# Memory denominators as 32 columns, the gate's last product through PSUM, the head mask from GpSimd ramps, and a new order

## The chip, the cores and the metric

The kernel runs on one core of a Trainium2 chip. Its time is the device time of one execution, in microseconds, and a kernel's time is the median of its runs. The engines are TensorE (PE, with its weight loads as PEld), VectorE (DVE), ScalarE (ACT), GpSimd (POOL) and SyncE (SP), which here only issues DMAs.

## What is computed

A block of two parts over 2048 rows of 512 values, in float32: attention with a compressed memory, then a gated FFN, each behind a layer norm and with a residual.

```python
x = A_x
h = x + _A_ref(_layernorm(x), A_wq, A_wk, A_wv, A_wo, A_beta)
h2 = h + _B_ref(_layernorm(h), B_w_gate, B_w_up, B_w_down)
```

The attention has 32 heads of 16 columns and 4 segments of 512 rows. Within a segment it is causal softmax attention. From the segments before it each head keeps a 16 x 16 memory M and a vector z:

```python
num = jnp.einsum("bhld,bhde->bhle", pq, M)          # pq = phi(q)
den = jnp.einsum("bhld,bhd->bhl", pq, z)[..., None] + 1e-6
o = g * (num / den) + (1.0 - g) * a_dot             # g = sigmoid(beta), one for each head
M = M + jnp.einsum("bhld,bhle->bhde", pk, vs)       # pk = phi(k)
z = z + jnp.einsum("bhld->bhd", pk)
```

The FFN is `(gelu(x @ w_gate) * (x @ w_up)) @ w_down`, with 1376 inner columns and the tanh form of gelu.

## The kernel before

**Units.** 8 heads (a chunk c of 128 columns) in one segment s are a unit: 16 units, each of two halves of 4 heads. For a unit, `qkv` projects Q and K (L888, for the first unit L898), splits them into a high part (ACT, L983) and a low part (DVE, L985), and copies both by DMA into the tiles stq and stk (L996, L1002), where a head's rows lie in the interleaved form that the passes read. `vproj` makes V for two chunks (L927, L940 for the first) in the tile vaug.

**Two passes.** For each half `pass_a` multiplies Q by K (L1123) and lets DVE take each row's largest value from PSUM (L1133, into nm). GpSimd splits these values into high and low (L1147, L1148), DVE turns them into rows by four 32 x 32 transposes (L1154, `turn`), and a DMA writes them into stq, so that `pass_b`'s product (L1177) comes with the maximum taken off. ACT exponentiates (L1183), GpSimd cuts the diagonal blocks (L1191), and PE multiplies by V in 32-column tiles (L1205).

**Memory.** `mup` (L1037, PE in 32-column tiles) forms pk times v and the sum of pk for a unit. `mask` (L1048, L1051) spreads that over the heads into the tile mb, multiplying by a constant head mask, mmask. Columns 0 to 127 of mb hold the memory; columns 128 to 159 hold the vector z of 8 heads, each repeated 4 times. GpSimd adds the unit before (L1058). `mem` uses it in segments 1 to 3, 12 times in all: `den` (L1073) multiplies mb's last 32 columns, as weights, by pq in four products of 128 columns, `inv` adds 1e-6, inverts and multiplies by the gate (L1079 to L1081), every fourth row of the result goes to DRAM and comes back spread over 128 partitions, and the numerators (L1091) are multiplied by it (L1096).

**Constants.** mmask is made at the start: two GpSimd ramps (L606, L608), and on DVE a copy to integers (L615), a bitwise and (L616), three subtractions over 32 partitions each (L618) and one comparison (L620).

**FFN.** Weights and activations are combined in blocks so that 7 products (L1466) stand for 8. `geglu` runs for two halves s of the rows: ACT squares (L1484), DVE L1486, ACT tanh (L1488), DVE L1490 (tanh + 1, times the gate), DVE L1492 (half of that, times u), then ACT and GpSimd split the result and `down` multiplies by w_down (L1530), added up by DVE (L1538). For s = 0 u is a PSUM bank; for s = 1 it is a tile in SBUF.

**The order.** Every step is recorded as an operation of one engine with a planned length. A table of 4741 numbers, ORDER, gives the order in which all of them are issued; buffers come from pools in that order (all 8 PSUM banks are one pool, 35 row tiles another), and the planner refuses an order in which none is free. A planned length decides nothing at run time: it served to lay out the order. For DVE it is `n / 960 + 0.072` us. Each engine, and SP's queue, works strictly in its order.

The functions that the change touches:

Of the kernel before, what the change touches and what calls it, by code (L numbers as in the profile page):

```python
# [1632 lines left out]
```

## Time and profile before

| | us |
|---|---|
| median of 3 runs | 765.69 (765.08 to 765.71) |
| the profiled execution | 764.84 |
| its span, first to last instruction | 762.9 |
| PE, PEld busy | 739.2, 583.7 |
| DVE, ACT, POOL busy | 610.5, 503.3, 479.6 |

The profile is of one execution. The page gives shares and groups; the trace behind it answers for windows, for the timeline, for waits (who waited for whom) and for the chain, which is followed back from the last instruction through whatever released each one. Matmuls overlap, so the mean of one is longer than what it takes of PE; the busy time of a group, divided by its steps, is the better price. An entry such as `[4.46 <-DMA stq<-slot]` is idle time ahead of an instruction and what ended it. Line numbers are those of the kernel before; in the changed kernel the same lines stand two lower up to L1035 (L985 is L983, L1037 is L1035) and one or two higher behind `inv` (L1123 is L1124, L1154 is L1155, L1492 is L1494).

### The profile page before, as it was taken

The page shows a single profiled execution, that of the slowest core. Times are in us where ns is not written, and L with a number is a line of the kernel's source. Part 1 is how long each engine was busy: PE and PEld are TensorE (multiplying, and loading weights), DVE is VectorE, ACT ScalarE, POOL GpSimd, SP SyncE. Part 2 cuts the span into 40 slices and gives each one's busy share as a digit, 9 for nine tenths or more (in the row PEclk, how much of TensorE's full clock was granted, in tenths as well). Part 3 has the DMA queues.
Part 4 walks back from the last instruction along what each step waited for, and adds up shares of the span by engine and source line. Part 5 has one row for each costly group of instructions (what it writes and reads, how often), then busy time and mean ns, then how long its engine had stood idle before and what let it go on. Part 6 is the DMA issues. An engine that isn't in the chain of part 4 may idle for free.

```text
span 762.9 us, 17952 instructions
## 1 busy us (share of the span) xinstructions
PE 739.2 (97%) x6126; PEld 583.7 (77%) x6126; DVE 610.5 (80%) x1922; ACT 503.3 (66%) x1004; POOL 479.6 (63%) x748
## 2 busy tenths in 40 slices
PE   7799999999999999999999999999999999999998
PEld 6688778776878777676667788788887878888886
DVE  6899889999998899999997554875678765665576
ACT  5688887787876777867766456866586455464450
POOL 6244554544545565778676689866998378768731
PEclk9899999999999999999999999999999999999999
DMA  6465657546656677776667684442544252000002
GB/s 247 125 183 137 163 154 192 151 123 196 184 149 192 166 204 198 187 212 209 169 191 232 191 277 147 120 101 48 150 124 128 56 152 79 2 1 0 1 1 110
DMA packets 88394, 107.85 MB, mean 141 GB/s; under 512 B 29824, under 2 KB 40624, under 8 KB 88304
## 3 DMA queue, kind: packets, MB, share of 16 engines
q1 hardware_dynamic: 88000, 106.32, 49.0%
q8 instruction: 48, 0.79, 0.5%
q10 hardware_dynamic: 304, 0.39, 0.2%
q14 instruction: 42, 0.34, 0.2%
HBM read 57.02 MB, written 23.53 MB: 106 GB/s over the span
## 4 chain that ended last, share of the span: by engine, by line
PE 74%; DVE 17%; issue 3%; ACT 3%; DMA 2%; SPq 1%; POOL 0%; DVEq 0%; ACTq 0%; POOLq 0%
PE bank L1466 26%; PE bank L1530 14%; PE bank L888 8%; PE bank L1205 7%; PE bank L927 4%; PE bank L1123 4%; PE bank L1177 4%; DVE aside L1133 3%; PE bank L1278 3%; DVE bank L1133 3%; DVE mx L1154 1%; PE bank L1285 1%; PE bank L1091 1%; DVE slot L985 1%; DVE nm L1133 1%
## 5 line engine op out<-in xcount | busy, mean ns | idle before, releaser
L1183 ACT ACTIVATE row<-bank 128x512 f32<-128x512 f32 x306 | 164.7, 604 | 38.6 <-PE bank L1177 26.9
L1191 POOL TENSOR_SCALAR_AFFINE_SELECT row<-row 128x256 f32<-128x256 f32 (+1 forms) x306 | 105.2, 367 | 99.9 <-ACT row L1183 87.9
L1133 DVE CUSTOM_DVE_ANT_0 aside<-bank,amask 128x128 f32<-128x128 f32 (+2 forms) x384 | 142.0, 419 | 7.3 <-PE bank L1123 4.7
L888 PE MATMUL bank<-slot,slot 64*128 64x512 f32 x720 | 117.3, 408 | 0.0
L1466 PE MATMUL bank<-slot,slot 128*128 128x512 f32 (+1 forms) x381 | 103.3, 391 | 1.1 <-DVE row L1538 1.1
L1123 PE MATMUL bank<-stk,stq 64*128 64x256 f32 (+3 forms) x512 | 88.3, 337 | 6.8 <-DMA stq<-slot 4.5
L1133 DVE CUSTOM_DVE_ANT_0 bank<-bank,amask 128x512 f32<-128x512 f32 x128 | 86.4, 710 | 5.4 <-PE bank L1123 5.0
L1177 PE MATMUL bank<-stq,stk 64*128 64x512 f32 (+3 forms) x512 | 85.6, 337 | 1.4 <-DVE nm L1133 0.3
L1466 PEld LDWEIGHTS bank<-slot,slot 128*128 128x128 f32 (+1 forms) x381 | 69.9, 184 | 18.3 <-DVE row L1538 2.0
L1205 PE MATMUL bank<-row,vaug 128*32 128x128 f32 (+3 forms) x976 | 78.1, 437 | 3.6 <-DVE nm L1133 0.9
L888 PEld LDWEIGHTS bank<-slot,slot 64*128 64x128 f32 x720 | 76.0, 188 | 6.6 <-issue 0.8
L1538 DVE TENSOR_TENSOR row<-row,bank 128x512 f32<-128x512 f32 (+1 forms) x91 | 60.1, 676 | 22.6 <-PE bank L1530 22.5
L1123 PEld LDWEIGHTS bank<-stk,stq 64*128 64x128 f32 x512 | 60.0, 188 | 22.9 <-DVE nm L1133 7.7
L1436 POOL TENSOR_TENSOR slot<-row,slot 128x512 fp32r<-128x512 f32 (+3 forms) x56 | 63.4, 1141 | 21.9 <-ACT slot L1434 21.9
L1177 PEld LDWEIGHTS bank<-stq,stk 64*128 64x128 f32 x512 | 58.0, 184 | 16.8 <-DVE nm L1133 5.7
L1530 PE MATMUL bank<-slot,slot 128*128 128x512 f32 (+1 forms) x252 | 67.6, 391 | 0.9 <-DVE row L1490 0.6
L668 POOL TENSOR_TENSOR slot<-row,slot 128x512 fp32r<-128x512 f32 (+1 forms) x34 | 44.0, 1293 | 28.1 <-ACT slot L663 27.8
L1205 PEld LDWEIGHTS bank<-row,vaug 128*32 128x32 f32 x976 | 30.6, 109 | 39.2 <-issue 31.9
L1530 PEld LDWEIGHTS bank<-slot,slot 128*128 128x128 f32 (+1 forms) x252 | 47.1, 188 | 12.0 <-DVE row L1490 1.0
L927 PE MATMUL bank<-slot,slot 64*128 64x256 f32 x672 | 54.9, 284 | 0.0
L927 PEld LDWEIGHTS bank<-slot,slot 64*128 64x128 f32 x672 | 49.5, 186 | 2.0 <-issue 0.8
L1133 DVE DVE_READ_ACCUMULATOR2_ANT nm<- 128x1 f32 x512 | 50.0, 98 | 0.0
(254 smaller groups left out, 1660.5 us busy)
## 6 DMA issues: line engine op xcount, KB each, us to landing
stq<-slot SPq DMA_DIRECT2D x96, 128.0 KB
stk<-slot SPq DMA_DIRECT2D x94, 128.0 KB
row<-x SPq DMA_DIRECT2D x32, 256.0 KB
pv_dram<-row SPq DMA_DIRECT2D x31, 256.0 KB
row<-r_dram SPq DMA_DIRECT2D x27, 256.0 KB
row<-h_dram SPq DMA_DIRECT2D x22, 256.0 KB
row<-wg SPq DMA_DIRECT2D x17, 256.0 KB
row<-wd SPq DMA_DIRECT2D x17, 256.0 KB
```

The costliest lines, as they stand in the source:

```text
L888: return nc.tensor.matmul(pm[i].t, w[i].t[rows_of(r), wi, dc * P:(dc + 1) * P], XT[s][dc].t[rows_of(r), xi, :], start=(dc, wi, xi, ph) == ...
L927: return nc.tensor.matmul(pms[n].t[:, 256 * t:256 * t + 256], XT[s][dc].t[rows_of(r), xi, t0:t0 + P], whl[wi].t[rows_of(r), dc // 2, 256 * ...
L1123: nc.tensor.matmul(sa.t[:, c0:c0 + w], sq.t[own, p, i * P:(i + 1) * P], sk.t[own, p, 0:w], start=True, stop=True, tile_position=(64 * a, 0 ...
L1133: nc.vector.tensor_tensor_reduce(out=(sa.t[:, c0:c0 + w] if i > 2 else aside[:, turns[0]:turns[0] + w]), in0=sa.t[:, c0:c0 + w], in1=amask ...
L1177: nc.tensor.matmul(sc.t[:, c0:c0 + D - q0], sk.t[own, p, q0:q0 + P], sq.t[own, p, q0:D], start=True, stop=True, tile_position=(64 * a, 0), ...
L1183: act(w, prio, lambda sc=sc, e=e: nc.scalar.activation(e.t[:, :w], sc.t[:, :w], AF.Exp), [sc, vtab], [e])
L1191: nc.gpsimd.affine_select(v, v, pattern=pat + [[1, P]], compare_op=OP.is_ge, fill=0.0, base=0, channel_multiplier=-1)
L1205: nc.tensor.matmul(pv.t[32 * n:32 * n + 32, kb * P:D], va.t[:, 136 * kb + 17 * j:136 * kb + 17 * j + 32], e.t[:, lo:lo + D - kb * P], star ...
L1436: pool(0.14 + 2.13e-3 * (hi - lo), prio, lambda: nc.gpsimd.tensor_tensor(v.t[:, 1, :hi - lo], r.t[:, lo:hi], v.t[:, 0, :hi - lo].bitcast(F ...
L1466: nc.tensor.matmul(dst.t[:w], v.t[:, wi, c0 + j * w:c0 + (j + 1) * w], b[bk][j].t[:, xi, :], start=first and j == 0 and n == 0, stop=j == ...
L1530: nc.tensor.matmul(pm.t[:, cs], HH[p, f, s].t[:w, hi, t * P:(t + 1) * P], v.t[:w, wi, cs], start=f == fl[0] and n == 0, stop=f == fl[-1] a ...
L1538: dve(W_, prio, lambda a=a, pm=pm, cs=cs, to=to: nc.vector.tensor_tensor(to.t[:, cs], a.t[:, cs], pm.t[:, cs], op=OP.add), [pm, a], [to])
```

## The change

Denominators. mb has 8 columns for z in place of 32, and the product is turned round: pq is the weights, in 16 tiles of 32 columns, mb's 8 columns are what streams, and the result stands with the rows of x on the partitions and 4 x 8 columns beside each other. `inv` works on these 32 columns, multiplies by a gate that is now spread over all partitions (8 columns for each chunk), and turns the result by one transpose for the write to DRAM.

```diff
-    PZ = Pool_(many("z", 1, [P, P]))
+    PZ = Pool_(many("z", 2, [P, 32]))
-    PMB = Pool_(many("mb", 7, [P, 160]))
+    PMB = Pool_(many("mb", 7, [P, 136]))
-    gt = sb("gt", [P, 2, NCH])
+    gt = sb("gt", [P, 9, NCH])
...
             for t in range(4):
-                nc.tensor.matmul(pd.t[32 * t:32 * t + 32, 0:P], mb.t[:, P:160],
-                                 pq.t[:, t * P:(t + 1) * P], start=True, stop=True,
-                                 tile_position=(0, 32 * t), skip_group_check=True)
-        pe(0.22, prio, den, [pq, mb], [pd], acq=[z], head=0.03, tail=0.02, mode="c")
+                for i in range(4):
+                    q0 = t * P + 32 * i
+                    nc.tensor.matmul(pd.t[32 * i:32 * i + 32, 8 * t:8 * t + 8], pq.t[:, q0:q0 + 32],
+                                     mb.t[:, P:136], start=True, stop=True,
+                                     tile_position=(0, 32 * i), skip_group_check=True)
+        pe(0.25, prio, den, [pq, mb], [pd], acq=[z], head=0.03, tail=0.02, mode="c")
...
-            nc.vector.tensor_scalar(pd.t[:, 0:P], pd.t[:, 0:P], 1e-6, None, op0=OP.add)
-            nc.vector.reciprocal(pd.t[:, 0:P], pd.t[:, 0:P])
-            nc.vector.tensor_scalar(z.t, pd.t[:, 0:P], gt[:, 1, c:c + 1], None, op0=OP.mult)
-        dve(1500, prio, inv, [pd, vgt], [pd, z])
+            d = pd.t[:, 0:32]
+            nc.vector.tensor_scalar(d, d, 1e-6, None, op0=OP.add)
+            nc.vector.reciprocal(d, d)
+            by_t = d.rearrange("p (t j) -> p t j", t=4)
+            nc.vector.tensor_tensor(by_t, by_t, gt[:, None, 1:9, c].to_broadcast([P, 4, 8]), op=OP.mult)
+            nc.vector.transpose(z.t, d.rearrange("p (t j) -> p j t", t=4))
+        dve(560, prio, inv, [pd, vgt], [pd, z])
```

`mask` writes 4 columns for z where it wrote 16, twice for each unit; the loads of the gate values and the write to DRAM change their shapes to match.

Head mask. GpSimd makes the second ramp in four pieces of 32 partitions, each with its own start, so the three subtractions go; the integers are kept in a PSUM bank (vs) in place of a row tile.

```diff
+    vs = Val(PD)
...
-        nc.gpsimd.iota(jid, pattern=[[1, 8], [0, 17]], base=0, channel_multiplier=0,
-                       allow_small_or_imprecise_dtypes=True)
+        for r in range(4):
+            jid = vj.t[32 * r:32 * r + 32, 0:136].rearrange("p (j e) -> p j e", e=17)
+            nc.gpsimd.iota(jid, pattern=[[1, 8], [0, 17]], base=-(r % 2 + 4 * (r // 2)), channel_multiplier=0,
+                           allow_small_or_imprecise_dtypes=True)
...
-        hidi = vj.t[:, 136:272].bitcast(I32)
-        nc.vector.tensor_copy(hidi, hid)
+        hidi = vs.t[:, 0:136].bitcast(I32)
+        nc.vector.tensor_copy(hidi, vh.t[:, 0:136])
         nc.vector.tensor_scalar(hidi, hidi, 1, None, op0=OP.bitwise_and)
-        for r in range(1, 4):
-            nc.vector.tensor_scalar(jid[32 * r:32 * r + 32], jid[32 * r:32 * r + 32],
-                                    -float(r % 2 + 4 * (r // 2)), None, op0=OP.add)
...
-    dve(1500, -9.5, c_mmask, [vh, vj], [vmmask, vh, vj])
+    dve(640, -9.5, c_mmask, [vh, vj], [vmmask, vs])
```

Gate. For s = 1 the product of tanh + 1 and the gate is written back into the gate's PSUM bank, and the last product reads it there; that bank is held until then.

```diff
+            r = g_ if s else e
             dve(D, prio, lambda: nc.vector.scalar_tensor_tensor(
-                e.t[:w], e.t[:w], 1.0, g_.t[:w], op0=OP.add, op1=OP.mult), [g_], [e])
+                r.t[:w], e.t[:w], 1.0, g_.t[:w], op0=OP.add, op1=OP.mult), [g_, e], [r])
             dve(D, prio, lambda: nc.vector.scalar_tensor_tensor(
-                e.t[:w], e.t[:w], 0.5, u_.t[:w], op0=OP.mult, op1=OP.mult), [u_], [e])
+                e.t[:w], r.t[:w], 0.5, u_.t[:w], op0=OP.mult, op1=OP.mult), [u_, r], [e])
```

Planned lengths and order. Beside the new steps above, the turn is planned at 760 for 330, a row transpose of `layer_norm` at 600 for 512, the copies into stq and stk at 155 KB for 128, and the whole of ORDER is laid out anew. Its numbers say nothing to a reader; this is its kind:

```diff
-        dve(330, prio, turn, [m2], [mx])
+        dve(760, prio, turn, [m2], [mx])
...
-    6, 10, 8, 12, 5, 9, 7, 11, 84, 0, 1, 75, 14, 15, 16, 18, 72, 73, 4, 771, 2, 970, 13, 81, 17, 19, 28, 74,
```

What it moves, at three places. The first is DVE at the start, behind the last low halves of the first segment's input. slot_79 and slot_80 (slot_81 and slot_82 after) are Q and K of the first unit, bn and mv the sums of the second segment's layer norm. Before:

```order
L615 CAST row_109<-row_108 128x136
L616 TENSOR_SCALAR row_109<-row_109 128x136
L618 TENSOR_SCALAR row_109<-row_109 32x136 x3
L620 SCALAR_TENSOR_TENSOR mmask<-row_109 128x136
L724 BN_STATS bn_157<-row_118 128x6
L725 BN_AGGR mv_159<-bn_157 128x2
L724 BN_STATS bn_157<-row_120 128x6
L725 BN_AGGR mv_159<-bn_157 128x2
L713 TENSOR_SCALAR mv_160<-bn_158 128x1
L716 TENSOR_SCALAR bn_158<-bn_158 128x1
L985 SCALAR_TENSOR_TENSOR slot_79<-bank_71,slot_79 128x512
L985 SCALAR_TENSOR_TENSOR slot_80<-bank_72,slot_80 128x512
```

And now, on the same engine, from the last low half of the input (L855; L857 before, where it stood ahead of the small L713, now L711) to those of Q and K:

```order
L711 TENSOR_SCALAR mv_161<-bn_159 128x1
L855 TENSOR_TENSOR slot_76<-bank_70,slot_76 128x512
L714 TENSOR_SCALAR bn_159<-bn_159 128x1
L722 BN_STATS bn_158<-row_110 128x6
L723 BN_AGGR mv_160<-bn_158 128x2
L722 BN_STATS bn_158<-row_118 128x6
L723 BN_AGGR mv_160<-bn_158 128x2
L722 BN_STATS bn_158<-row_114 128x6
L723 BN_AGGR mv_160<-bn_158 128x2
L983 SCALAR_TENSOR_TENSOR slot_81<-bank_71,slot_81 128x512
L983 SCALAR_TENSOR_TENSOR slot_82<-bank_72,slot_82 128x512
```

The head mask now follows after four rows more on the same engine, and behind it the first pass:

```order
L767 TENSOR_SCALAR bank_67<-mv_160 128x4
L616 CAST bank_68<-row_106 128x136
L617 TENSOR_SCALAR bank_68<-bank_68 128x136
L618 SCALAR_TENSOR_TENSOR mmask<-bank_68,row_107 128x136
L773 RECIPROCAL ln_166<-ln_165 128x4
```

The whole mask has gone from ahead of the low halves of Q and K to behind them, and takes three instructions for six; three statistics stand ahead of those low halves where two stood. On ACT's queue the first two copies of K into stk (L1002) stood behind the high halves of Q and K with two activations between, one of them L719, which waits for DVE; now three stand between, L661, L907 and L661.

The second place is DVE near the end of attention, at the last of the 12 inversions (bank_68 before, bank_66 after, are the denominators; mx is what the turn writes). Before:

```order
L1079 TENSOR_SCALAR bank_68<-bank_68 128x128
L1080 RECIPROCAL bank_68<-bank_68 128x128
L1081 TENSOR_SCALAR z_138<-bank_68,gt 128x128
L545 COPY tock<-bank_72 128x1
L1154 STREAM_TRANSPOSE mx_156<-mm_155 32x32 x4
L545 COPY tock<-bank_65 128x1
```

And now:

```order
L545 COPY tock<-bank_65 128x1
L1155 STREAM_TRANSPOSE mx_157<-mm_156 32x32 x4
L545 COPY tock<-bank_69 128x1
L1079 TENSOR_SCALAR bank_66<-bank_66 128x32
L1080 RECIPROCAL bank_66<-bank_66 128x32
L1082 TENSOR_TENSOR bank_66<-bank_66,gt 128x32
L1083 STREAM_TRANSPOSE z_139<-bank_66 128x32
```

The turn stood behind the inversion and now stands ahead of it; the inversion has 32 columns and one instruction more.

The third place is PE at the first denominators (mb is the memory, vaug is V). Before:

```order
L888 MATMUL bank_65<-slot_90,slot_84 128x512
L1123 MATMUL bank_70<-stk_95,stq_100 128x512
L1123 MATMUL bank_72<-stk_95,stq_100 128x512
L1073 MATMUL bank_67<-row_123,mb_145 32x128 x4
L1205 MATMUL bank_66<-row_101,vaug_140 32x512
```

And now:

```order
L1206 MATMUL bank_66<-row_122,vaug_141 32x256
L1206 MATMUL bank_66<-row_114,vaug_141 32x256
L1072 MATMUL bank_69<-mb_146,row_118 32x8 x16
L1035 MATMUL bank_68<-vaug_141,row_125 32x34 x16
L1206 MATMUL bank_72<-row_105,vaug_141 32x512
```

4 products of 128 columns became 16 of 8, with the operands in each other's place; here they stand among other products in 32-column tiles, where before they opened such a stretch. Over the whole program PE goes 43 times from 64-row tiles to 32-column tiles, and went 40 times before. In the FFN the two DVE rows of the gate (L1492 and L1494 in the changed kernel) stand directly behind each other in 15 of the 22 gated tiles of s = 1.

More of the change, by code (lines that the diff above doesn't have):

```diff
@@ L600, in infini_geglu @@
     vj = Val(PJ)
+    vs = Val(PD)
     def c_iota():
         hid = vh.t[:, 0:136].rearrange("p (j e) -> p j e", e=17)
-        jid = vj.t[:, 0:136].rearrange("p (j e) -> p j e", e=17)
         nc.gpsimd.iota(hid, pattern=[[0, 8], [0, 17]], base=0, channel_multiplier=1,
                        allow_small_or_imprecise_dtypes=True)
-        nc.gpsimd.iota(jid, pattern=[[1, 8], [0, 17]], base=0, channel_multiplier=0,
-                       allow_small_or_imprecise_dtypes=True)
-    pool(1.0, -9.5, c_iota, [], [vh, vj])
+        for r in range(4):
+            jid = vj.t[32 * r:32 * r + 32, 0:136].rearrange("p (j e) -> p j e", e=17)
+            nc.gpsimd.iota(jid, pattern=[[1, 8], [0, 17]], base=-(r % 2 + 4 * (r // 2)), channel_multiplier=0,
+                           allow_small_or_imprecise_dtypes=True)
+    pool(1.7, -9.5, c_iota, [], [vh, vj])
     def c_mmask():
-        hid, jid = vh.t[:, 0:136], vj.t[:, 0:136]
-        hidi = vj.t[:, 136:272].bitcast(I32)
-        nc.vector.tensor_copy(hidi, hid)
+        hidi = vs.t[:, 0:136].bitcast(I32)
+        nc.vector.tensor_copy(hidi, vh.t[:, 0:136])
         nc.vector.tensor_scalar(hidi, hidi, 1, None, op0=OP.bitwise_and)
-        for r in range(1, 4):
-            nc.vector.tensor_scalar(jid[32 * r:32 * r + 32], jid[32 * r:32 * r + 32],
-                                    -float(r % 2 + 4 * (r // 2)), None, op0=OP.add)
-        nc.vector.scalar_tensor_tensor(mmask.rearrange("p j e -> p (j e)"), hidi, 2.0, jid,
+        nc.vector.scalar_tensor_tensor(mmask.rearrange("p j e -> p (j e)"), hidi, 2.0, vj.t[:, 0:136],
                                        op0=OP.mult, op1=OP.is_equal)
-    dve(1500, -9.5, c_mmask, [vh, vj], [vmmask, vh, vj])
+    dve(640, -9.5, c_mmask, [vh, vj], [vmmask, vs])
     def c_ident():
@@ L830, in layer_norm @@
             q = Val(PN)
-            dve(D, prio, lambda t=t, q=q: nc.vector.transpose(q.t, rows[t].t), [rows[t]], [q])
+            dve(600, prio, lambda t=t, q=q: nc.vector.transpose(q.t, rows[t].t), [rows[t]], [q])
             for a in range(4):
@@ L997, in qkv @@
                                               hl.t[64 * h:64 * h + 64, part].bitcast(F32)),
-                            [hl] + zeros, [dst], kb=128, chain=True)
+                            [hl] + zeros, [dst], kb=155, chain=True)
                         continue
@@ L1005, in qkv @@
                     else:
-                        dma(moved + 0.2 + h, lambda move=move: move(nc.sync), [hl] + zeros, [dst], kb=128,
+                        dma(moved + 0.2 + h, lambda move=move: move(nc.sync), [hl] + zeros, [dst], kb=155,
                             chain=True)
@@ L1051, in mask @@
                 nc.vector.tensor_tensor(
-                    mb.t[:, P:160].rearrange("p (a b j r) -> p a b j r", a=2, b=2, j=2)[:, :, :, j],
-                    m[:, None, :, 16:17].to_broadcast([P, 2, 2, 4]),
-                    pick[:, :, :, 16:17].to_broadcast([P, 2, 2, 4]), op=OP.mult)
+                    mb.t[:, P:136].rearrange("p (a b j) -> p a b j", a=2, b=2)[:, :, :, j],
+                    m[:, None, :, 16].to_broadcast([P, 2, 2]), pick[:, :, :, 16], op=OP.mult)
         dve(330, later + 0.8, mask, [pu, vmmask], [mb])
@@ L1072, in den @@
             for t in range(4):
[L1073 to L1082 removed]
+                for i in range(4):
[4 more added lines that the diff above has]
+        pe(0.25, prio, den, [pq, mb], [pd], acq=[z], head=0.03, tail=0.02, mode="c")
+        def inv():
+            d = pd.t[:, 0:32]
[5 more added lines that the diff above has]
+        dve(560, prio, inv, [pd, vgt], [pd, z])
         dma(prio, lambda: nc.sync.dma_start(
[L1084 to L1085 removed]
+            r_dram[U, 1].rearrange("j (t i q) -> i (j t) q", t=4, i=4), z.t), [z], [vr], kb=16)
         om = OM[U] = Val(POM)
@@ L1376, in infini_geglu @@
     pool(0.1, 0.5, lambda: nc.gpsimd.memset(gt, 0.0), [], [vgt, vgz])
-    for i, ap in enumerate([[[0, 16], [NCH, 8], [1, NCH]], [[0, 4], [NCH, 8], [1, NCH]]]):
+    for i, ap in enumerate([[[0, 16], [NCH, 8], [1, NCH]], [[0, P], [1, 8 * NCH]]]):
         dma(1, lambda i=i, ap=ap: nc.sync.dma_start(
-            gt[0:P:4 if i else 1, i], bass.AP(tensor=beta.tensor, offset=beta.offset, ap=ap)), [*XT[1], vgz], [vgt],
+            (gt[:, 1:9] if i else gt[:, 0]), bass.AP(tensor=beta.tensor, offset=beta.offset, ap=ap)), [*XT[1], vgz], [vgt],
             kb=2, chain=True)
-    act(8, 1, lambda: nc.scalar.activation(gt, gt, AF.Exp, scale=-1.0), [vgt, vtab], [vgt])
+    act(36, 1, lambda: nc.scalar.activation(gt, gt, AF.Exp, scale=-1.0), [vgt, vtab], [vgt])
     def c_gate():
```

2 lines of the change are left out of this document (removed), and 507 rows, old and new, of the table ORDER.

## The prediction

> **What bounds the kernel now.** I read the page first: how busy each engine is, and which engines the chain that ended last runs through.
>
> ```profile
> PE 739.2 (97%) x6126; PEld 583.7 (77%) x6126; DVE 610.5 (80%) x1922; ACT 503.3 (66%) x1004; POOL 479.6 (63%) x748
> PE 74%; DVE 17%; issue 3%; ACT 3%; DMA 2%; SPq 1%; POOL 0%; DVEq 0%; ACTq 0%; POOLq 0%
> ```
>
> PE (TensorE) is busy for 739.2 of 762.9 us, so no more than 23.7 us of visible PE idle time can be won; DVE holds 17% of the chain. An average over stages hides where, so I cut the span into windows at the places where the program changes its nature: start, first head passes, attention, FFN (columns: the window, its length, then PE, PEld, DVE, ACT, POOL busy, granted clock, DMA share, GB/s).
>
> ```profile
> 0.00:24.00 24.00, 19.44 (x108) 16.46 (x108) 17.68 (x36) 11.28 (x24) 13.11 (x32) 1.00 0.57 203
> 24.00:28.00 4.00, 0.00 (x0) 0.00 (x0) 2.13 (x9) 3.66 (x13) 2.26 (x4) 0.79 0.91 211
> 28.00:34.00 6.00, 5.70 (x36) 5.12 (x38) 4.39 (x23) 4.75 (x9) 0.00 (x0) 0.57 0.78 233
> 34.00:60.00 26.00, 25.16 (x333) 20.97 (x331) 23.80 (x110) 21.18 (x46) 11.76 (x26) 1.00 0.53 147
> 60.00:400.00 340.00, 331.74 (x4018) 251.56 (x4014) 321.77 (x1348) 259.79 (x531) 198.28 (x438) 1.00 0.64 177
> 400.00:759.00 359.00, 356.86 (x1641) 289.42 (x1642) 239.94 (x400) 202.69 (x387) 254.21 (x250) 1.00 0.34 100
> ```
>
> Four readings. The FFN (400 to 759) is PE alone: 2.1 us idle, DVE at 67%. Attention (60 to 400) is nearly two-sided: PE 97.6%, DVE 321.77 of 340, 94.6%, so work taken off DVE counts there. From 34 to 60 DVE is at 92%. And between 24 and 28 PE does nothing, while the granted clock falls to 0.79 and then 0.57. The timeline shows what came before that gap and what ended it; its next to last row is of the chain.
>
> ```profile
> 14.47 0.16 DVE L713 TENSOR_SCALAR mv<-bn 128x1 f32<-128x1 f32 x1
> 14.61 0.93 DVE L615 CAST row<-row 128x136 int32<-128x136 f32 x1
> 15.57 1.22 DVE L616 TENSOR_SCALAR row<-row 128x136 int32<-128x136 int32 x1
> 16.80 3.92 DVE L618 TENSOR_SCALAR row<-row 32x136 f32<-32x136 f32 x3
> 17.92 5.91 PE L940 MATMUL bank<-slot,slot 128*128 128x256 f32 x48
> 17.89 1.09 ACT L983 ACTIVATE slot<-bank 128x512 fp32r<-128x512 f32 x2 [1.10 <-PE bank L898]
> 20.75 0.30 DVE L620 SCALAR_TENSOR_TENSOR mmask<-row 128x136 f32<-128x136 int32 x1
> 22.68 1.28 DVE L985 SCALAR_TENSOR_TENSOR slot<-bank,slot 128x512 fp32r<-128x512 f32 x2
> 24.63 3.54 DMA stq<-slot
> ...
> 28.30 1.33 PE L1123 MATMUL bank<-stk,stq 64*128 64x384 f32 x8 [4.46 <-DMA stq<-slot]
> ```
>
> The head mask (L615 to L620) holds DVE from 14.61 to 21.05, 6.4 us, three subtractions on 32 partitions taking 3.92 of it. ACT has the high halves of Q and K at 18.98, but DVE forms the low halves (L985) only at 22.68; SP's copies into stq queue behind them, the last is issued at 24.63 and lands 3.54 us later. PE ends the V projection at 23.83 and waits 4.46 us.
>
> **The change, part by part.**
>
> *Head mask.* DVE loses the three subtractions and its first two steps go to a PSUM bank; the new order also puts all of it behind the low halves. Ahead of these now stand three statistics of the next layer norm, as cheap as here:
>
> ```profile
> 21.69 0.18 DVE L725 BATCH_NORM_AGGREGATE mv<-bn 128x2 f32<-128x6 f32 x1
> 21.79 0.66 DVE L724 BATCH_NORM_STATS2 bn<-row 128x6 f32<-128x512 f32 x1
> 22.97 0.61 ACTq L1002 DMA_DIRECT2D stk<-slot  x1
> 9.22 0.50 POOL L873 COPY tick<-row 128x1 f32<-128x1 f32 x1 [5.51 <-ACT row L782]
> 3.36 0.35 POOL L608 IOTA row<- 128x136 f32 x1
> ```
>
> After the last of the input's low halves (about 15.3, since the small L713 of 14.47 now stands ahead of it) they take 3 x 0.84 = 2.5 us, to 17.8; so DVE is free when ACT finishes, and the low halves stand at about 19.9. SP's third stq copy and the stk copy then go by about 21; the two stk copies on ACT's queue now stand behind three activations of some 0.6 us (as L983's) and go at 20.9 and 21.5. The last copy took 3.54 us; so all has landed near 25.0 and PE waits 1.2 us, not 4.46: **-3.2**. Bounds: -2.0 (copies of one burst share the rings, landing near 26.2) and -4.5 (no gap). The mask's own steps, now 0.3 to 0.9 us on DVE, lie in that wait. GpSimd's three more ramps, 3 x 0.35 us, lie in the 5.51 us that it waits for L782.
>
> The gap has a second price: clock 0.57 over 28 to 34 is 6 x 0.43 = 2.6 us of PE time lost. DVE is the next engine late there (4.39 of 6, then 23.80 of 26), so I count **-0.7** of it, bounds 0 and -2.6. [...]
>
> *Denominators.* The old step and its nearest rows:
>
> ```profile
> L1079 DVE TENSOR_SCALAR bank<-bank 128x128 f32<-128x128 f32 x12 | 3.6, 301 | 0.7 <-PE bank L1073 0.7
> L1080 DVE RECIPROCAL bank<-bank 128x128 f32<-128x128 f32 x12 | 11.6, 966 | 0.4
> L1081 DVE TENSOR_SCALAR z<-bank,gt 128x128 f32<-128x128 f32 x12 | 4.2, 351 | 0.4
> L1238 DVE RECIPROCAL cd<-cd 128x32 f32<-128x32 f32 x14 | 4.8, 344 | 0.0
> L1051 DVE TENSOR_TENSOR mb<-bank,mmask 128x16 f32<-128x16 f32 x22 | 3.6, 165 | 0.0
> L1154 DVE STREAM_TRANSPOSE mx<-mm 32x32 f32<-32x32 f32 x120 | 23.8, 198 | 2.4 <-POOL mm L1148 0.9
> L1073 PE MATMUL bank<-row,mb 128*32 128x128 f32 x96 | 5.0, 279 | 0.0
> L1037 PE MATMUL bank<-vaug,row 128*32 128x34 f32 x384 | 5.7, 199 | 0.0
> L1037 PEld LDWEIGHTS bank<-vaug,row 128*32 128x32 f32 x384 | 5.2, 111 | 1.1 <-issue 0.3 <-ACT vaug L1183 0.2
> 147.79 0.98 DVE bank L1080
> 367.62 0.98 DVE bank L1080
> ```
>
> Before: 301 + 966 + 351 = 1.62 us of DVE for each of 12 units. After: an addition over 32 columns (between 165 for 16 and 301 for 128; 0.19), a reciprocal (344), a product (0.19), a transpose (198): 0.92. Off DVE: 12 x 0.70 = 8.4 us. How much reaches the end? Two of 12 reciprocals lie on the chain, which gives 2/12 x 8.4 = -1.4 as the small end; the whole 8.4 is the large end, if DVE bound all of attention. Between them I take half, **-4.2**: DVE is nearer to full (94.6%) than the chain's two entries suggest, PE has 8.3 us idle there to give, and at several places the turn (L1154, four transposes, on whose result PE's next pass waits through a copy) stood right behind the reciprocal. What is late next is PE.
>
> PE pays: 16 matmuls of 8 columns for 4 of 128. L1037 is the same shape, 16 matmuls with 32-column weights (32 records a step): 5.7 / 12 = 0.475 us a step against 5.0 / 12 = 0.417. So 12 x 0.06, **+0.7**; bounds 0 (8 columns for 34) and +1.4. [...]
>
> The mask's products shrink from 16 to 4 columns (24 x at most 0.03 us), the second PZ buffer and the denominators' write by 128 rows of 128 B cost no engine time; the gate values go from 8 to 36 columns once. Together nothing: about 1 us of slack work among 340.
>
> *Gate's last product.* The second half's product read two SBUF tiles; the forms before:
>
> ```profile
> L1492 DVE SCALAR_TENSOR_TENSOR row<-row,row 128x512 f32<-128x512 f32 (+1 forms) x14 | 13.2, 945 | 0.2
> L1492 DVE SCALAR_TENSOR_TENSOR row<-row,vaug 128x512 f32<-128x512 f32 x6 | 7.4, 1231 | 0.1
> L1492 DVE SCALAR_TENSOR_TENSOR row<-row,bank 128x512 f32<-128x512 f32 (+1 forms) x20 | 13.7, 684 | 5.9 <-PE bank L1466 5.7
> PE bank L1466 <- DVE row L1538: 1.1, 2, 0.8
> PE bank L1530 <- DVE row L1490: 0.6, 1, 0.6
> PE bank L1530 <- DVE row L1492: 0.2, 1, 0.2
> ```
>
> With one operand in PSUM it should take 684: 14 x 0.26 + 6 x 0.55 = 7 us off DVE. But PE is the bound there and waits 1.9 us on DVE in all: **-0.5**, bounds -2.1 and, since the gate's bank is now held until that product, a wait in its place (a rival below).
>
> *Order.* The planner's price of a turn goes from 330 to 760, by its formula 0.42 to 0.86 us; the trace has 4 x 198 = 0.79. So 32 turns were planned some 0.4 us short, 13 us on an engine that is 94.6% busy. The new order should stall less, but it moves thousands of rows; it also adds three changes of PE into column mode (40 to 43). I take **0**, bounds -4 and +5.
>
> **The sum.** -3.2 - 0.7 - 4.2 + 0.7 - 0.5 + 0 = -7.9 us. The profiled execution took 764.84 (span 762.9); 764.84 - 7.9 = 756.9. The median of the runs shown, 765.69, lies 0.85 above it, so on that scale **757.8**.
>
> **Rivals.** About 0.2%, 1.5 us, is what a measurement of this kernel can tell from no change.
>
> *Attention was DVE's.* All 8.4 come off, the start gives -3.2 - 2.6 and the FFN -2.1: -15.6 with the +0.7, 750.1. For it: DVE at 94.6% and above 90% from 34 on. Against: PE at 97.6% beside it.
>
> *Only the start.* PE takes up nothing in attention; -3.2 + 0.7 = -2.5, and 763.2. For it: 74% of the chain is PE. Against: 8.3 us of PE idle there.
>
> *The order eats it.* +5 from the order and the small ends (-2.0, -1.4, +0.7): 2 us, about 768; a milder case lies within 0.2% of before. The orders' shared skeleton speaks against it.
>
> *Slower: the gate's bank.* In each of 22 gated tiles PE's next product into that bank waits for the extra product. At 0.684 us each that is +15, 773; it decides when PE waits over 7.9 / 22 = 0.36 us a tile. Against: in 15 of 22 tiles the product stands directly behind the one that writes the bank.
>
> *Slower: small matmuls do not overlap.* If each of 32 records of a denominator cost its own weight load, 111 ns, a step takes 3.6 us: +38. It decides above (0.417 + 7.9 / 12) / 32 = 34 ns a record. L1037 at 15 ns speaks against it.
>
> **How the numbers follow.** Forecast (754 to 762) 0.52; attention was DVE's 0.17; only the start 0.17; within 0.2% of before 0.07; slower 0.07 (order 0.03, bank 0.02, matmuls 0.02). Faster is the first three, 0.86. The range reaches from the DVE case's 750 to 764, past the start case; it leaves out half of the DVE case's far side and the last 0.14.
>
> **What would show it.** Right: PE idle behind the V projection near 1.2 us and no clock below 0.9 after it; inversion steps near 0.92 us and denominators under 0.55 us on PE; DVE in attention some 8 us less busy; the product at 0.68; a span near 755. Wrong: a gap still over 3 us (the copies, not the mask, were late); attention as long as before with DVE idle (it was PE's); PE waits on the product in the FFN.

## The result and the profile after

| | before | after |
|---|---|---|
| median, us | 765.59 (765.08 to 765.71, 4 runs) | 752.64 (751.42 to 755.26, 4 runs) |
| ratio to before, 95% interval | 1 | 0.9837 (0.9808 to 0.9865) |
| profiled execution, its span, us | 764.84, 762.9 | 751.42, 749.7 |

The change makes the kernel 12.5 us faster by the ratio (10.3 to 14.7 by its interval), where 7.9 was forecast. The median, 752.64, lies 1.4 us below the 754 to 762 to which the forecast gave 0.52, and within its range of 750 to 764. Two runs of kernels further down stand far out, 804.56 us with mask and denominators in the old order and 1792.27 us with two more reciprocals: the ratios leave them out, the medians count them in. First the engines over the whole span, from the page of after:

```profile
PE 732.3 (98%) x6414; PEld 580.5 (77%) x6414; DVE 589.2 (79%) x1931; ACT 502.0 (67%) x1004; POOL 476.6 (64%) x751
```

DVE has lost 21.3 us. PE has 288 records of matmuls more, and yet 6.9 us less of busy time: that is worth keeping in mind. Up to 2.6 us of it is the half clock of before (6 x 0.43 between 28 and 34), under which L888's matmuls of 64 x 512 took 619 ns each, against 405 between 34 and 60; the rest says that a part of what the page calls busy was waiting. The windows of after, cut at the same stages (columns as before: window, length, PE, PEld, DVE, ACT, POOL, granted clock, DMA share, GB/s):

```profile
24.00:28.00 4.00, 3.79 (x32) 3.08 (x34) 3.35 (x17) 3.98 (x11) 2.13 (x2) 1.00 0.99 308
28.00:34.00 6.00, 5.85 (x67) 4.80 (x66) 5.93 (x30) 5.90 (x14) 1.38 (x4) 1.00 0.69 206
34.00:60.00 26.00, 25.43 (x337) 20.80 (x338) 24.93 (x119) 23.54 (x53) 11.95 (x34) 1.00 0.45 116
60.00:390.00 330.00, 324.20 (x4249) 247.69 (x4241) 306.36 (x1332) 252.68 (x515) 195.72 (x432) 1.00 0.66 178
390.00:746.00 356.00, 355.23 (x1632) 289.63 (x1631) 232.82 (x399) 202.48 (x389) 249.04 (x244) 1.00 0.35 103
```

The hole between 24 and 28 is gone, and with it the lowered clock (0.79, then 0.57 before). The timeline of the start shows the mask in its new place, and the gap that is left ahead of the first pass:

```profile
16.67 1.09 ACT L981 ACTIVATE slot<-bank 128x512 fp32r<-128x512 f32 x2 [0.72 <-PE bank L896]
17.30 1.29 DVE L983 SCALAR_TENSOR_TENSOR slot<-bank,slot 128x512 fp32r<-128x512 f32 x2 [0.47 <-ACT slot L981]
19.64 0.29 DVE L616 CAST bank<-row 128x136 int32<-128x136 f32 x1
19.96 0.31 DVE L617 TENSOR_SCALAR bank<-bank 128x136 int32<-128x136 int32 x1
20.38 0.30 DVE L618 SCALAR_TENSOR_TENSOR mmask<-bank,row 128x136 f32<-128x136 int32 x1
24.21 0.92 PE L1124 MATMUL bank<-stk,stq 64*128 64x512 f32 x7 [1.60 <-DMA stk<-slot]
```

The low halves (L983) wait for ACT now, not for the mask; the mask takes 1.0 us in place of 6.4; PE waits 1.60 us for the copies. The groups of the new denominators and of the gate's product in after (mean ns of one behind the busy time):

```profile
L1080 DVE RECIPROCAL bank<-bank 128x32 f32<-128x32 f32 x12 | 4.4, 367 | 0.4
L1082 DVE TENSOR_TENSOR bank<-bank,gt 128x32 f32<-128x32 f32 x12 | 2.6, 217 | 0.4
L1083 DVE STREAM_TRANSPOSE z<-bank 128x32 f32<-128x32 f32 x12 | 2.6, 217 | 0.4
L1079 DVE TENSOR_SCALAR bank<-bank 128x32 f32<-128x32 f32 x12 | 2.3, 192 | 0.0
L1494 DVE SCALAR_TENSOR_TENSOR row<-bank,row 128x512 f32<-128x512 f32 x14 | 9.6, 689 | 0.3
L1494 DVE SCALAR_TENSOR_TENSOR vaug<-bank,row 128x512 f32<-128x512 f32 x4 | 2.8, 691 | 0.1
```

An inversion takes 192 + 367 + 217 + 217 = 993 ns, 1.62 us before. On PE the small products stand in two groups, which differ in nothing but the name of a buffer:

```profile
L1072 PE MATMUL bank<-mb,row 128*32 128x8 f32 x352 | 5.0, 178 | 0.2 <-DVE nm L1134 0.2
L1072 PE MATMUL bank<-mb,vaug 128*32 128x8 f32 x32 | 0.4, 179 | 0.0
```

5.4 / 12 = 0.45 us a step, against 0.417 before. To see where the 13 us came from, the span is cut at three points of the timeline: the first matmul of the first pass a, the first product of the FFN (L1467 in after), and PE's last. Before: 28.30, then 362.1 of attention, then 368.9 of FFN. After: 24.21, 356.4, 365.5. So 4.1 us came at the start, 5.7 in attention and 3.4 in the FFN; the attention stretch of before also holds its half clock, those 2.6 us. The diff has four parts, and each of the three stretches could owe its gain to an edit or to the new order. That is what the experiments have to separate.

### The profile page after: what moved, and what is told of

Read it like the earlier page. It is cut to its first block, busy times and chain, and to the rows that moved or that the text cites. A ratio compares the mean times of both kernels' runs of the same rounds, so it can differ in the third digit from the quotient of the medians.

```text
span 749.7 us, 18550 instructions
## 1 busy us (share of the span) xinstructions
PE 732.3 (98%) x6414; PEld 580.5 (77%) x6414; DVE 589.2 (79%) x1931; ACT 502.0 (67%) x1004; POOL 476.6 (64%) x751
## 5 line engine op out<-in xcount | busy, mean ns | idle before, releaser
L1184 ACT ACTIVATE row<-bank 128x512 f32<-128x512 f32 x312 | 167.4, 608 | 41.8 <-PE bank L1178 39.5
L886 PE MATMUL bank<-slot,slot 64*128 64x512 f32 x720 | 115.0, 402 | 0.1
L1467 PE MATMUL bank<-slot,slot 128*128 128x512 f32 (+1 forms) x381 | 102.8, 391 | 0.2 <-ACT row L1225 0.2
L1124 PE MATMUL bank<-stk,stq 64*128 64x128 f32 (+3 forms) x512 | 85.3, 335 | 3.0 <-DMA stk<-slot 1.6
L1540 DVE TENSOR_TENSOR row<-row,bank 128x512 f32<-128x512 f32 (+1 forms) x85 | 56.5, 677 | 38.3 <-PE bank L1532 37.6
L1467 PEld LDWEIGHTS bank<-slot,slot 128*128 128x128 f32 (+1 forms) x381 | 70.4, 185 | 16.4 <-issue 0.4
L1206 PE MATMUL bank<-row,vaug 128*32 128x512 f32 (+3 forms) x996 | 77.5, 436 | 1.7 <-DVE nm L1134 0.9
L1437 POOL TENSOR_TENSOR slot<-row,slot 128x512 fp32r<-128x512 f32 (+3 forms) x49 | 54.3, 1111 | 21.5 <-ACT slot L1435 20.4
L666 POOL TENSOR_TENSOR slot<-row,slot 128x512 fp32r<-128x512 f32 (+1 forms) x31 | 39.9, 1292 | 13.0 <-ACT slot L661 13.0
L1532 PE MATMUL bank<-slot,slot 128*128 128x512 f32 (+1 forms) x180 | 48.1, 390 | 0.0
L1474 ACT ACTIVATE row<-bank 128x512 f32<-128x512 f32 (+1 forms) x50 | 29.4, 593 | 25.2 <-PE bank L1467 22.6
```

What stands on the lines that cost most here:

```text
L886: return nc.tensor.matmul(pm[i].t, w[i].t[rows_of(r), wi, dc * P:(dc + 1) * P], XT[s][dc].t[rows_of(r), xi, :], start=(dc, wi, xi, ph) == ...
L1124: nc.tensor.matmul(sa.t[:, c0:c0 + w], sq.t[own, p, i * P:(i + 1) * P], sk.t[own, p, 0:w], start=True, stop=True, tile_position=(64 * a, 0 ...
L1184: act(w, prio, lambda sc=sc, e=e: nc.scalar.activation(e.t[:, :w], sc.t[:, :w], AF.Exp), [sc, vtab], [e])
L1206: nc.tensor.matmul(pv.t[32 * n:32 * n + 32, kb * P:D], va.t[:, 136 * kb + 17 * j:136 * kb + 17 * j + 32], e.t[:, lo:lo + D - kb * P], star ...
L1437: pool(0.14 + 2.13e-3 * (hi - lo), prio, lambda: nc.gpsimd.tensor_tensor(v.t[:, 1, :hi - lo], r.t[:, lo:hi], v.t[:, 0, :hi - lo].bitcast(F ...
L1467: nc.tensor.matmul(dst.t[:w], v.t[:, wi, c0 + j * w:c0 + (j + 1) * w], b[bk][j].t[:, xi, :], start=first and j == 0 and n == 0, stop=j == ...
```

## The experiments

"Old order" is the ORDER of before, "new order" that of after with its planned lengths. Differences between two kernels are taken between their ratios to before, times 765.5 us, with the two intervals added as squares.

### The edits under the old order

Three kernels: before with the head mask edit, with the denominators' edit, and with both. Their edits are those lines of the diff, unchanged. The gate's product was not tried there.

> The kernel before, in its own order, with the head mask edit alone (ramps in four pieces, three subtractions gone, integers in a PSUM bank). Theory (the edits carry the gain, each in its own place): the mask on DVE falls from 6.4 to about 1.0 us, the low halves of Q and K go at about 18.9 and not 22.7, PE's gap ahead of the first pass falls from 4.46 to about 1.3 us and the half clock behind it goes; the time is 3 to 5 us under before's (761 to 763). Rival (the new order carries it): the mask stands ahead of the low halves as before, and the copies into stk stand where they stood, so the gap stays over 2.5 us and the time is at most 2 us under before's.

Measured: 760.22, ratio 0.9933 (0.9920 to 0.9946), 5.1 us faster. The timeline of this kernel:

```profile
14.72 0.30 DVE L618 SCALAR_TENSOR_TENSOR mmask<-bank,row 128x136 f32<-128x136 int32 x1
17.54 1.29 DVE L983 SCALAR_TENSOR_TENSOR slot<-bank,slot 128x512 fp32r<-128x512 f32 x2 [0.80 <-ACT slot L981]
24.58 0.73 PE L1121 MATMUL bank<-stk,stq 64*128 64x384 f32 x6 [1.66 <-DMA stq<-slot]
```

The mask is done at 15.0 and in nobody's way; the first pass starts 3.7 us earlier than before, the gap is 1.66. The theory holds for the start: the edit carries it, in the old place too. One part of it fails: the half clock behind the gap did not go (0.69 between 24 and 28, see the last section).

> The kernel before, in its own order, with the denominators' edit alone (8 columns of z, 16 small products, inversion on 32 columns). Theory (attention was DVE's for more than half of the time): 12 x 0.62 = 7.5 us less of DVE, PE about 0.3 us more in all, first to last pass some 4 to 5 us shorter, the time 4 to 5 us under before's. Rival (the order carries attention's gain): PE finds nothing else to do at the places where DVE is now early, and the time is 0 to 2 us under before's.

> The kernel before, in its own order, with the head mask edit and the denominators' edit. Theory: the sum of the two alone, 7 to 10 us under before's; the new order and the gate's product are left with 3 to 6 us. Rival (the order carries it): at most 4 us under before's, and the order is left with 9.

Measured: 763.90, ratio 0.9985 (0.9974 to 0.9996) for the denominators alone, 1.1 us faster; 760.09, ratio 0.9931 (0.9917 to 0.9945) for both, which is 0.2 +- 1.5 us under the mask alone. For the denominators alone the rival holds, and my theory falls. Both together lie 5.3 us under before, between the theory's 7 to 10 and the rival's 4; since the mask alone gives 5.1, the denominators again add next to nothing. One row for attention from the windows of each, first before, then the denominators alone:

```profile
28.00:390.00 362.00, 353.60 (x4306) 272.39 (x4308) 340.56 (x1450) 276.34 (x566) 204.52 (x450) 0.99 0.63 175
```

```profile
28.00:388.00 360.00, 352.13 (x4592) 273.27 (x4594) 333.14 (x1461) 276.41 (x567) 204.02 (x450) 1.00 0.64 176
```

DVE lost 7.4 us (340.56 to 333.14), and the stretch only 2: DVE's idle time rose from 21.4 to 26.9. Its waits for the first pass's products, with both edits in:

```profile
DVE aside L1134 <- PE bank L1124: 7.1, 10, 3.5
DVE bank L1134 <- PE bank L1124: 6.7, 15, 0.9
```

With the mask edit alone it waited 5.9 and 4.4 us for the same, before 4.7 and 5.0. So in an order that places PE's passes for inversions of 1.6 us, much of what an inversion saves comes back as a wait; with the denominators alone the waits are spread over several products (5.6 and 5.0 us on these two lines).

### Old steps under the new order

> The kernel after, in its new order, with the gate's last product as before (second operand in SBUF). Theory (the product gave about 3 us in the feed-forward part, where PE's waits for DVE went): 2 to 3 us over after's, PE idle in the feed-forward part again near 2 us, DVE 7 us busier there. Rival (the feed-forward part gained by the order, or by PE's own cadence): within 0.7 us of after's, with the product at 0.95 to 1.2 us beside a busy PE.

Its edit is the third part of the diff undone. Measured: 755.45, ratio 0.9869 (0.9852 to 0.9886). Two things follow. Against after, the gate's product is worth 2.4 +- 2.6 us, which the ratio alone does not resolve; the FFN does. From its first product to PE's last it takes 367.85 us here and again 367.85 in the next kernel, which also has the old product in the new order, while the eight kernels with the new product in the new order, after among them, lie between 365.5 and 365.7. So 2.3 us is the gate's. PE waits 1.3 us in one place again:

```profile
PE bank L1467 <- DVE row L1539: 1.3, 1, 1.3
```

Against the kernel with mask and denominators in the old order, the new order is worth 4.7 +- 1.7 us with these steps: 1.1 in the FFN (368.97 there), the rest in attention.

> The steps of the kernel before (long head mask, denominators over 128 columns, gate's product from SBUF) in the order of the kernel after, with its planned lengths. So that the old denominators fit, two z buffers of 128 columns stand where there was one, and the scratch that the row minima write to is 5 x 128 columns for 6 x 128. Theory (the order is worth 4.6 us by itself in attention, as it was with the mask and denominators edited, and hides most of the mask behind the low halves): 756 to 759. Rival (the order was laid out for the short steps and stalls with the long ones): 763 or more.

Measured: 773.33, ratio 1.0110 (1.0094 to 1.0126). It is slower than before, and the theory falls: the order is not worth 4.6 us by itself. How much of the loss is the smaller scratch, the control below has to say.

> The kernel after with the denominators as before (4 products of 128 columns, inversion over 128 columns, two z buffers of 128 columns, scratch of the row minima 5 x 128 columns for 6 x 128), in the new order. Theory (attention is bound by PE, and DVE's 7.5 us were nearly all slack): 0 to 1.5 us over after's, 752.6 to 754. Rival (the new order is what makes use of DVE's relief): 3.5 us or more over after's, 756 or more.

Measured: 768.28, ratio 1.0040 (1.0024 to 1.0056), 15.6 us over after's median. The rival holds by far, and by more than DVE's 7.5 us can explain one for one, which calls for the control below. PE's waits in attention, in this kernel:

```profile
PE bank L1175 <- DVE nm L1131: 2.3, 7, 0.7
PE bank L1121 <- DVE nm L1131: 2.1, 5, 0.6
PE bank L1175 <- DVE z L1079: 1.3, 2, 0.8
PE bank L1121 <- DVE z L1079: 0.9, 2, 0.6
```

Both passes (L1121 and L1175) wait for DVE's minima and for the inversion's last step. In after the same list has 0.5 and 0.4 for the minima and 0.3 for the inversion.

> The kernel after with the head mask as before (one ramp, three subtractions, integers in SBUF), in the new order, so behind the low halves of Q and K. Theory (at the start the place counts, not the length): the gap ahead of the first pass stays at 1.6 to 2.5 us and the time is 0 to 1.5 us over after's. Rival (the length counts: the row sums and the first row minima behind the mask come 5 us late): 3 to 5 us over after's, 756 to 758.

Measured: 755.39, ratio 0.9858 (0.9838 to 0.9879), 1.6 +- 2.7 us over after. The first pass starts at 24.59 behind a gap of 2.17 us, so the theory holds as far as this can tell: behind the low halves the long mask no longer delays it. It costs a second gap of 0.81 us inside that pass.

### Doses

Three kernels, after with one thing added. The first is the control, the second adds to DVE, the third to PE:

```diff
-    aside = sb("aside", [P, 6 * P])
+    aside = sb("aside", [P, 5 * P])
-                        turns[0] = 3 * P - turns[0]
+                        turns[0] = 2 * P - turns[0]
```

```diff
             d = pd.t[:, 0:32]
+            for _ in range(2):
+                nc.vector.reciprocal(z.t, amask[:, 0:32])
```

```diff
-            for t in range(4):
+            for t in [*range(4), *range(4)]:
                 for i in range(4):
                     q0 = t * P + 32 * i
```

> The kernel after with one thing changed: the scratch that the row minima write to is 5 x 128 columns, its two places 256 columns apart and not 384, so that a minimum over 384 columns overlaps with the place of the one before or behind it. It is the control to the two runs that needed this scratch. In the run with the old denominators in the new order these minima kept DVE busy for 147.4 us (379 of them) against 142.2 (384). Theory (overlapping writes make DVE start the next one later, and in the new order DVE sets the pace): 5 to 8 us over after's, and the old denominators alone would then be worth the other 8 to 10. Rival (the scratch is nothing): within 1.5 us of after's, and all 15.6 us were the denominators'.

Measured: 762.66, ratio 0.9953 (0.9935 to 0.9971), 8.9 +- 2.6 us over after. The theory holds, and the time lies a little above its 5 to 8. The minima over 128 to 384 columns in this kernel:

```profile
L1134 DVE CUSTOM_DVE_ANT_0 aside<-bank,amask 128x128 f32<-128x128 f32 (+2 forms) x384 | 149.1, 420 | 12.2 <-PE bank L1124 4.2 <-ACT row L1184 1.0 <-ACT vaug L955 0.6
```

And in after:

```profile
L1134 DVE CUSTOM_DVE_ANT_0 aside<-bank,amask 128x128 f32<-128x128 f32 (+2 forms) x384 | 142.2, 419 | 6.8 <-PE bank L1124 4.4 <-ACT row L1184 0.7 <-ACT vaug L955 0.6
```

One lasts as long in both, 420 and 419 ns, but together they hold DVE 6.9 us longer, and DVE is idle ahead of them for 12.2 us in place of 6.8: neighbours overlap less. Two neighbours over 384 columns show it, first with the small scratch, then in after:

```profile
67.53 0.55 DVE L1134 CUSTOM_DVE_ANT_0 aside<-bank,amask 128x384 f32<-128x384 f32 x1
68.13 0.56 DVE L1134 CUSTOM_DVE_ANT_0 aside<-bank,amask 128x384 f32<-128x384 f32 x1
```

```profile
65.51 0.56 DVE L1134 CUSTOM_DVE_ANT_0 aside<-bank,amask 128x384 f32<-128x384 f32 x1
65.98 0.56 DVE L1134 CUSTOM_DVE_ANT_0 aside<-bank,amask 128x384 f32<-128x384 f32 x1
```

The second starts 0.60 us after the first where their places share columns, 0.47 where they don't. Of 260 such pairs, one minimum right behind another, 91 share columns in the small scratch: there the second starts 122 ns later (median), in the other 169 no later than in after. That is 11 us of DVE, for 8.9 us of time.

So the old denominators' share in the new order is the difference of the two kernels with this scratch, 1.0040 - 0.9953 = 0.0087, 6.7 +- 1.8 us, for about 7.7 us of DVE.

> The kernel after with two more reciprocals of 128 x 32 ahead of each inversion's steps, written to z, which the transpose then writes over: 12 x 0.71 = 8.5 us more of DVE, nothing else. Theory (in the new order DVE sets the pace of attention, at about 1 us of time for 1 us of DVE): 6 to 9 us over after's, 759 to 762. Rival (DVE has slack there, as the denominators' edit under the old order suggests, where 7.5 us of DVE were worth 1.5): at most 2 us over after's.

Measured: 760.34, ratio 0.9927 (0.9903 to 0.9950), 6.9 +- 2.8 us over after. The dose itself, by its group:

```profile
L1080 DVE RECIPROCAL z<-amask 128x32 f32<-128x32 f32 x24 | 8.4, 349 | 0.5
```

The attention row of this kernel's windows, and below it that of after:

```profile
24.00:387.00 363.00, 352.37 (x4598) 271.19 (x4598) 339.34 (x1489) 277.33 (x568) 203.31 (x450) 1.00 0.62 171
```

```profile
24.00:380.00 356.00, 349.45 (x4592) 270.35 (x4594) 331.80 (x1467) 277.58 (x573) 202.28 (x449) 1.00 0.65 174
```

DVE has 7.5 us more, the stretch is 7 longer, and DVE's idle time stays (23.7 and 24.2). PE's busy time rises by 2.9 us, though it was given nothing more to do.

> The kernel after with the 16 small products of the denominators issued twice, the second set writing the same values over the first: 12 x 0.45 = 5.4 us more of PE, nothing more elsewhere. Theory (attention is bound by PE): 4.5 to 6 us over after's, 757 to 759. Rival (PE has slack where the denominators stand, DVE sets the pace): at most 2 us over after's.

Measured: 753.67, ratio 0.9850 (0.9828 to 0.9872), 1.0 +- 2.8 us over after. The dose on PE, by its groups:

```profile
L1072 PE MATMUL bank<-mb,row 128*32 128x8 f32 x704 | 8.4, 178 | 0.1
L1072 PE MATMUL bank<-mb,vaug 128*32 128x8 f32 x64 | 0.7, 178 | 0.0
```

That is 9.1 us for 5.4, so 3.7 us more and not the 5.4 that I had counted. The theory's 4.5 us at least falls. One for one, 3.7 us would still lie at the edge of the interval; the runs at a mean clock of 0.999 or 1.000 are closer: 752.30, 752.41 and 753.67 here, 751.42, 751.78 and 753.51 for after, 0.6 us between the middle ones. (The profiled execution, 757.71, had a mean clock of 0.995 and is not typical.) So PE, 98% busy on the page, has slack where the denominators stand, and DVE, 93% busy in attention, has nearly none there.

### A lighter kernel, and one too many

If 1 us of DVE costs 0.7 to 1 us of time in attention, taking more off it should pay. The inversion's sum and gate go together, and one small mask product does the work of two:

```diff
-            nc.vector.tensor_scalar(d, d, 1e-6, None, op0=OP.add)
-            nc.vector.reciprocal(d, d)
-            nc.vector.tensor_tensor(by_t, by_t, gt[:, None, 1:9, c].to_broadcast([P, 4, 8]), op=OP.mult)
+            nc.vector.scalar_tensor_tensor(by_t, by_t, 1e-6, gt[:, None, 1:9, c].to_broadcast([P, 4, 8]),
+                                           op0=OP.add, op1=OP.mult)
+            nc.vector.reciprocal(d, d)
...
-        nc.vector.reciprocal(gt, gt)
+        nc.vector.reciprocal(gt[:, 0], gt[:, 0])
```

> The kernel after with less work for DVE: the sum with 1e-6 and the gate go in one step ahead of the reciprocal (the gate's columns for it stay 1 + exp(-beta), without their own reciprocal), and the two small mask products of 4 columns become one of 8. By the durations of after's groups that is 12 x 0.19 + 12 x 0.15 = 4.1 us less of DVE. Theory (DVE sets the pace at about 1 us for 1 us): 2.5 to 4 us under after's, 748.5 to 750. Rival (PE is the bound as soon as DVE is as short as in after): within 1.2 us of after's.

Measured: 750.27, ratio 0.9783 (0.9758 to 0.9808), 4.1 +- 2.9 us under after. It is the fastest of all the kernels here. Its attention row and its engines:

```profile
23.00:375.00 352.00, 347.10 (x4592) 269.00 (x4590) 328.55 (x1440) 276.34 (x568) 202.80 (x449) 1.00 0.64 175
```

```profile
PE 730.7 (98%) x6414; PEld 579.6 (78%) x6414; DVE 585.4 (79%) x1907; ACT 502.0 (67%) x1004; POOL 477.5 (64%) x751
```

DVE is 3.3 us shorter in attention, and so is the stretch from its first pass to the FFN (353.2 for 356.4); the profiled execution also started its first pass 1.6 us earlier, as its V projection ended sooner. The last kernel goes further and turns the row maxima with one transpose:

```diff
-            for i in range(4):
-                own = slice(32 * i, 32 * i + 32)
-                nc.vector.transpose(mx.t[:, own], m2.t[own].bitcast(F32).rearrange("p a r i -> p (a r i)"))
+            nc.vector.transpose(mx.t, m2.t.bitcast(F32).rearrange("p a r i -> p (a r i)"))
...
+            for k in range(4):
+                nc.sync.dma_start(sq.t[3:P:32].bitcast(F32).rearrange(
+                    "x p (i k q) -> x p i k q", k=4, q=32)[:, :, :, k], mx.t[32 * k:32 * k + 32])
```

> The lighter kernel (one step fewer in the inversion, one mask product of 8 columns), and beside it the turn of the row maxima in one transpose of 128 x 32 in place of four of 32 x 32, with four copies of 32 partitions each into stq in place of one of 32 rows of 512 B. DVE loses 32 x (4 x 0.199 - 0.217) = 18.5 us; SP issues 96 copies more, and their packets are 128 B. Theory (DVE sets the pace, but PE is near to its own bound: 4.9 us of idle are left to see in attention): 3 to 8 us under the lighter kernel's, 742 to 747. Rival (the second pass of each quarter waits for the last of four copies, each issued some 0.5 us behind the one before): 32 x 1 us against what DVE gives back, 755 or more.

Measured: 769.43, ratio 1.0032 (1.0011 to 1.0053), 19 us over the lighter kernel. The rival holds. PE's longest wait in attention, here:

```profile
PE bank L1181 <- DMA stq<-mx: 12.0, 8, 3.3
```

and in the lighter kernel:

```profile
PE bank L1179 <- DMA stq<-mx: 0.3, 1, 0.3
```

DVE is relieved by 19 us (transposes 25.5 to 6.6 us in all) and nobody can use it: the second pass waits for the copy of the maxima. Part of the 19 us of time goes with a lower clock: the runs have a mean clock of 0.987 to 0.995, those of the lighter kernel 0.998 to 1.000. DVE sets the pace only as long as nothing else on the way from one pass to the next gets longer.

## Why the prediction was right, and where it was not

Put together from before to after, the medians fall 765.44, 760.22 (mask), 760.09 (denominators, old order), 755.45 (new order), 752.64 (gate): -5.2, -0.1, -4.6, -2.8. The forecast had -3.9, -3.5, 0 and -0.5. The direction was right, and so was most of each operation's cost. That the sum came within 5 us is in part luck: the order and the gate's product gave 6.9 us more than forecast and the mask 1.3, the denominators 3.4 less. The shares depend on the order in which the parts are added here, as the start shows.

*Start.* The step was right. The low halves went as soon as ACT was done, the copies had landed at 24.2 (25.0 forecast), the gap is 1.60 (1.2), a gain of 4.1 us for the 3.2 forecast. Either half of it does it alone: with the short mask in its old place the first pass starts at 24.58, with the long mask in its new place at 24.59. Part of the rest is not the change: the V projection ends anywhere between 21.7 and 24.3 in the profiled executions of these kernels, whatever the edit, and with the short mask in the new order the first pass starts between 22.6 and 25.4.

*Clock.* Right for after, where it stays at 1.00, but that was luck: see the last section. The -0.7 is not measured by itself. The mask edit in the old order speaks for a small price: its run at a mean clock of 0.998 took 760.22 us, three at 1.000 took 760.07 to 760.88.

*Denominators.* The cost of each operation was right (0.99 us an inversion for 0.92 forecast; DVE in attention 340.56 to 331.80, 8.8 us less; 0.45 us a step on PE for 0.475). The step that failed is "I take half, -4.2". Half is no property of the edit. Under the old order it gives 0.2 to 1.1 us, because PE's passes stand where they stood; under the new one 6.7. The chain's two of 12 reciprocals, my small end of -1.4, was the better reading for the old order.

*Order.* The step that failed is "I take 0". It is worth -4.7 +- 1.7 with the short steps. With the old steps it is worth nothing good: 8.4 us slower than before, of which the scratch may be all (estimate: 8.9 us, if it costs as much there as in after). So order and denominators are one term, not two: each without the other gives little or loses, both together some 5 us, of which 1.1 are the order's in the FFN. I had priced them apart.

*PE's share.* PE's +0.7 for the small products was too much: the step takes 0.4 us more of PE in all, and twice as many of them cost 1.0 +- 2.8 us of time. The rival of matmuls that do not overlap decides above 34 ns a record; 32 records in 0.45 us are 14 ns each. In the trace of after they start in fours, mostly 7 ns apart within four and 12 ns from four to four (medians); which record goes to which tile the trace does not say.

*Gate.* The product takes 690 ns as forecast, and the bank's longer hold costs nothing that can be seen. The term was too small: -0.5 for 2.3 us in the FFN. I took part of the 1.9 us of PE's visible waits, and even the bound of -2.1, all of PE's idle time there, was short of 2.3. All of PE's idle time in the FFN fell from 2.3 to 0.95 us between the two kernels; the other 1 us lies inside "busy", where no list of waits shows it.

*The rivals.* "Attention was DVE's", to which I gave 0.17, is what the doses show of the new order; its sum of 750.1 was closer than mine. It is not what held before, where DVE's relief turned into waits for PE, and its terms were not right either: it took the full 2.6 us for the clock and nothing for the order.

## What to carry to other kernels

When every engine's queue is laid out ahead, an edit that shortens a step and the order that uses it are to be priced together: without a new order the gain ends as a wait on another engine, and the new order with an old length can stall, as it did with the old denominators. Which engine sets the pace is told by a dose, some microseconds of harmless work on one engine, better than by busy shares: here the one at 98% had slack at the place of the dose (3.7 us more of it cost 1.0 +- 2.8) and the one at 93% had not (7.5 us cost 6.9 +- 2.8). A kernel that cannot take an old step for lack of memory needs its own control, since the smaller scratch alone (8.9 +- 2.6 us) cost about as much as the step that was under test (6.7 +- 1.8).
